# Expert token places resized: 800, 800, then 832, 800, 800, 768, 768, 768 by size

## The chip, the cores and the metric

The kernel runs on one core of one Trainium2 chip. The metric is the device time of one execution in microseconds (us); less is better. Before the change the median of three runs is 593.02 us (591.11 to 594.56).

## The reference, cut to what matters

Two stages follow each other. The first is a linear-attention recurrence over 768 steps for 4 batches and 8 heads of width 48; its output, 3072 tokens of 384 numbers, is the input `x` of the second. The second is a mixture of 8 experts:

```
logits = x @ w_gate
noisy_logits = logits + log1p(exp(x @ w_noise)) * noise
top2 = the two largest experts of each token, weights by a softmax over the two
for e in range(8):
    h = np.maximum(x[mask] @ w1[e], 0.0)          # 384 -> 1024
    out[mask] += top2_w * (h @ w2[e])             # 1024 -> 384
```

So 6144 pairs of token and expert are spread over 8 experts, 768 on average. The numbers per expert depend on the data. For the inputs that the reference draws with its default seed, its own routing gives 791, 781, 778, 777, 779, 765, 726 and 747 for experts 0 to 7.

## The kernel before, in words

The attention works on 24 tiles of 128 tokens; routing (logits, top two, the place of each token within its expert) follows in two groups of 13 and 11 tiles and is interleaved with it. From some 145 us on, the experts run one after the other.

Each expert has a fixed number of places. Tokens are gathered into these places by an indirect DMA from `xd` (the attention's output in DRAM), so every expert computes its places whether a token fills them or not. Experts 0 and 1 are handled as they are numbered, because their lists are ready early. The other six are sorted by token count on the chip (`ranks`, L905) and handled largest first; I call the eight positions **slots** 0 to 7. `N_TAIL` (L84) and `NS` (L87) give the places: six tiles of 128 for each slot, and for the first `8 - NS` slots a seventh, narrow tile (the **tail**) of 64 or 32.

A slot is worked in two chunks: chunk 0 has tiles 0 to 2, chunk 1 has tiles 3 to 5 and the tail where there is one (`CHUNKS1`, `CHUNKS2`). I write (slot, chunk), so (5,1) is the second chunk of slot 5. Each chunk goes through:

- `xgather` (L967): one indirect DMA per tile, issued by GpSimd, reads the tokens' rows.
- `spread` (L987): for slots 2 to 7, 16 DMAs on SP's queue rearrange the gathered rows into `xq`.
- `xT` (L1026): transposes the rows (slots 0 and 1 on TensorE at L1044, slots 2 to 7 on VectorE at L1037) and splits them into a high part `xh` (ScalarE, L1046) and a low part `xl` (VectorE, L1047).
- `p1` (L1053), the first matrix: for each of 8 blocks of hidden units (f = 0 to 7) nine matmuls at L1071 into one PSUM tile `ph`, 72 per chunk. The weights are the stationary operand, 128x128; the tokens of the whole chunk are the moving operand, so a matmul has 384, 416 or 448 columns. ScalarE (L1075) and VectorE (L1077) evict `ph` into `hb` for the full tiles and into `ht` for the tail.
- `p2` (L1083), the second matrix, tile by tile. A full tile takes 24 matmuls at L1107. A tail takes 16, eight each at L1098 and L1100; there the tokens are the stationary operand and the 384 outputs the moving columns. ScalarE copies the result out (L1115; for a tail L1102, with a VectorE add at L1103).
- `emit_out` (L1118): weighs by the gate, adds what the token's other expert gave (`pv`, gathered by `pgather`, L978) and scatters the rows to `out` by an indirect DMA (L1130).

The order of work on every engine is written out by hand: the loop at L1370 emits `p1` of a chunk with the next chunk's `spread` and gate work between its blocks, then `p2` with the next chunk's `xT` and weight loads between its tiles. In `p1` of a slot's last chunk, `w_p1` (L346) converts the next slot's weights; in `p2`, `w_p2` (L357) loads more. While chunk (0,1) runs, leftover routing work sits between its blocks: `one` (L624), whose matmuls L615 yield expert 1's list; `rows` (L805) turns the list into row numbers `GR` at L810; `tokens` (L812) follows, then `ranks`, `places` and `half` for the sorted six.

Tokens beyond an expert's places are counted in `tile_counts` (L939) against `cap`. If any count is above zero, the branch at L1433 redoes the excess with a slow loop over all experts (`slow_expert`, L872), which reads each expert's two weight matrices again.

Of the kernel before, what the change touches and what calls it, by code (L numbers as in the profile page):

```python
# [41 lines left out]
ESP = 2  # L42
# [12 lines left out]
def kernel(  # L55
# [14 lines left out]
    nc = tc.nc  # L70
    B, H, S, D = r.shape
    N, E = noise.shape
# [8 lines left out]
    CAP = 832  # L81
    NM = 6
    TAIL = CAP - NM * 128
    N_TAIL = (TAIL,) * 3 + (TAIL // 2,) * 3  # L84
    CHUNKS1 = ((0, 1, 2), (3, 4, 5, 6))
    CHUNKS2 = ((0, 1, 2), (3, 4, 5))
    NS = 2  # L87
    WMAX = 3 * 128 + TAIL
    EARLY = 384
    LS = 4096  # L90
# [141 lines left out]
    cap = const.tile([1, E], F32, name="cap")  # L232
# [21 lines left out]
    def consts_a():  # L254
        nc.vector.tensor_scalar(ltri, idif, 0.0, None, op0=ALU.is_gt)
        nc.gpsimd.memset(ones_b, 1.0)
        nc.gpsimd.memset(acc, 0.0)
        for t in vd + Z:
            nc.gpsimd.memset(t[:, :, D:], 0.0)
        for t in xs:  # L260
            nc.gpsimd.memset(t[:, DM:], 0.0)
        nc.gpsimd.iota(ie, pattern=[[1, E]], base=0, channel_multiplier=0, allow_small_or_imprecise_dtypes=True)
        nc.vector.tensor_scalar(ier, ie, -1.0, float(E), op0=ALU.mult, op1=ALU.add)
        nc.vector.tensor_scalar(ie_n[:, 0, :], ie, float(LS), None, op0=ALU.mult)
        nc.gpsimd.memset(dl, 0.0)
        nc.gpsimd.memset(cap, float(CAP))
        nc.gpsimd.memset(cap[:, 3:], float(NM * 128 + TAIL // 2))
        nc.gpsimd.memset(cap[:, E - NS:], float(NM * 128))
        nc.vector.tensor_copy(pid[:, 0, :], ie[:1])
        nc.gpsimd.iota(im, pattern=[[1, 128]], base=0, channel_multiplier=0)  # L270
        nc.gpsimd.iota(ij, pattern=[[LS // 128, E], [1, NJ]], base=0, channel_multiplier=0)
        nc.gpsimd.iota(pcol, pattern=[[0, 1]], base=0, channel_multiplier=1, allow_small_or_imprecise_dtypes=True)
        nc.gpsimd.iota(thi, pattern=[[1, NT]], base=1, channel_multiplier=0, allow_small_or_imprecise_dtypes=True)

        nc.vector.tensor_copy(imp, im)
        nc.vector.tensor_copy(ijp, ij.rearrange("p e j -> p (e j)")[:, :NJ])
# [213 lines left out]
    def xtrans(i):  # L490
        pt = psum.tile([128, ND, 128], F32, name="ptx", tag="py0")
        for d in range(ND):
            nc.tensor.transpose(pt[:, d, :], X[i][:, d * 128:(d + 1) * 128], ident)  # L493
        t = att_pool[0].tile([128, ND, 128], F32, name="xT", bufs=LB)
        nc.scalar.activation(t, pt, AF.Copy)
        XT[i] = t
# [3 lines left out]
    def logits(i):  # L500
        g = [i >= a for a, _ in GROUPS].count(True) - 1
        j = i - GROUPS[g][0]
        if j == 0:
            LG[g] = att_pool[0].tile([128, GB, 2 * E], F32, name="lg")
        if j % LB < LB - 1 and i + 1 < GROUPS[g][1]:
            return
        m = j % LB + 1
        pl = psum.tile([128, 2, 128], F32, name="pl", tag="pt", bufs=2)
        for d in range(ND):
            for a in range(m):  # L510
                nc.tensor.matmul(pl[32 * a:32 * a + 32, 0, :], wg[:, d, :], XT[i - m + 1 + a][:, d, :],  # L511
                                 start=(d == 0), stop=(d == ND - 1), skip_group_check=True)
        ys = att_pool[0].tile([128, 128], F32, name="ys", bufs=1)
        nc.scalar.activation(ys[:32 * m], pl[:32 * m, 0, :], AF.Copy)
        PL[i] = pl, ys, m

    def logits_b(i):
        if i not in PL:
            return
        pl, ys, m = PL.pop(i)  # L520
        g = [i >= a for a, _ in GROUPS].count(True) - 1
        j = i - GROUPS[g][0]
        nc.tensor.transpose(pl[:, 1, :32 * m], ys[:32 * m], ident[:32 * m, :32 * m])
        nc.scalar.activation(LG[g][:, j - m + 1:j + 1, :],
                             pl[:, 1, :32 * m].rearrange("p (a b) -> p a b", b=32)[:, :, :2 * E], AF.Copy)
# [413 lines left out]
    def tile_counts(cnt, capped):  # L939

        nt = const.tile([1, E], F32, name="nt")
        if capped:
            nc.vector.tensor_sub(nt, cnt, cap)
            cnt = nt
        nc.vector.tensor_scalar(nt, cnt, 127.0, None, op0=ALU.add)
        nc.vector.tensor_add(nt[:, 0:1], nt[:, 0:1], ie_n[:1, 0, 0:1])
        nc.vector.tensor_scalar(nt, nt, 0.0, 1.0 / 128.0, op0=ALU.max, op1=ALU.mult)
        nc.vector.tensor_scalar(nt, nt, -127.0 / 256.0, 12582912.0, op0=ALU.add, op1=ALU.add)
        nc.vector.tensor_scalar(nt, nt, -12582912.0, None, op0=ALU.add)
        nc.vector.tensor_scalar(nt, nt, float(NCH), float(NCH), op0=ALU.mult, op1=ALU.min)  # L950
        nc.vector.tensor_copy(tab[:, :E], nt)
        mx = const.tile([1, 1], F32, name="mx")
        nc.vector.tensor_reduce(mx, nt, AX.X, ALU.max)
        nc.vector.tensor_add(mx, mx, bad)
        nc.vector.tensor_copy(tab[:, E + 1:E + 2], mx)


    def tw(e, t):
        return N_TAIL[e] if t == NM else 128

    XG, XH, HH, PV, OT, scat_of = {}, {}, {}, {}, {}, {}
    def chunks(e):
        return CHUNKS1 if e < E - NS else CHUNKS2

# [175 lines left out]


    consts_a()
    uterm_a(0)
    prep_k(1)
# [225 lines left out]
    for s in range(1, len(seq)):  # L1370
        e, ci = seq[s]
# [61 lines left out]
    with tc.If(any_r > 0):  # L1433
        thr = slow.tile([128, E], F32, name="thr")
        for e in range(E):
            nc.vector.memset(thr[:, e:e + 1], float(CAP if e < 3 else NM * 128 + (TAIL // 2 if e < E - NS else 0)))
        bad_r = nc.values_load(tab[:, E:E + 1], min_val=0, max_val=1)
        with tc.If(bad_r > 0):
            att_pool[0] = slow
            eye = slow.tile([D, D], F32, name="eye")  # L1440
            nc.vector.tensor_copy(eye, ident[:D, :D])
            one_d = slow.tile([D, 1], F32, name="one_d")
            nc.vector.memset(one_d, 1.0)
            with tc.For_i(0, B, 1) as b:
                with tc.For_i(0, H, 1) as h:
                    slow_head(b, h, slow, eye, one_d)
            nc.sync.dma_start(out.rearrange("(q p) d -> p q d", p=128),
                              zrow[:, None, :].to_broadcast([128, N // 128, DM]))
            nc.vector.memset(acc, 0.0)
            nc.vector.memset(ie_n[:, 0, 0:1], 0.0)  # L1450
            for i in range(NT):
                c, b = divmod(i, B)
                X[i] = slow.tile([128, DM], F32, name="xs")
                nc.sync.dma_start(X[i], xd[i * 128:(i + 1) * 128, :DM])
                xtrans(i)
                logits(i)
                logits_b(i)
                for g in range(len(GROUPS)):
                    if GROUPS[g][1] == i + 1:
                        for _ in route(g, False):  # L1460
                            pass
            pc = pwarm[:, 432:432 + E]
            nc.tensor.matmul(pc, ones_b, acc, start=True, stop=True)
            tile_counts(pc[:1], False)
            nc.vector.memset(tab[:, E:E + 1], 1)
            nc.vector.tensor_copy(pid[:, 0, :], ie[:1])
            nc.vector.memset(thr, 0.0)
        gov = slow.tile([128, E * NT], F32, name="gov")
        for e in range(E):
            g = slow.tile([128, 2, NT], F32, name="ge")  # L1470
            nc.vector.tensor_scalar(thr[:, e:e + 1], thr[:, e:e + 1], float(e * LS), None, op0=ALU.add)
            nc.vector.tensor_scalar(g, SLI, thr[:, e:e + 1], None, op0=ALU.is_ge)
            nc.vector.scalar_tensor_tensor(g, SLI, float((e + 1) * LS), g, op0=ALU.is_lt, op1=ALU.mult)
            nc.vector.tensor_mul(g, g, GTS)
            nc.vector.tensor_add(gov[:, e * NT:(e + 1) * NT], g[:, 0], g[:, 1])
        with tc.For_i(0, E, 1) as e:
            slow_expert(e, slow, gov)
# [29 lines left out]
```

## Time and profile before

| | before |
|---|---|
| runs, us | 593.02, 591.11, 594.56 |
| span of the profiled execution, first to last instruction, us | 590.2 |
| TensorE busy (matmul / weight load) | 572.8 us (97%) / 537.6 us (91%) |
| VectorE, ScalarE, GpSimd busy | 364.3, 254.4, 275.0 us |
| L1071, first matrix, 1152 matmuls | three groups of some 132 us each |
| L1107, second matrix, 1152 matmuls | 199.8 + 129.0 us |
| DMA | 85.45 MB, mean 145 GB/s |

The profile gives one execution and its span; a time of that execution beside its span isn't given, so the span stands beside the runs. The span is 2.8 us under their median. Matmuls are pipelined and their ends are modelled: a matmul's own duration includes latency, and the pitch from one start to the next says what it costs. The lists by line say where the time sits; the chain of waits says which of it sets the end.

### The profile page before, as it was taken

How to read it: one execution, taken by the hardware profiler on the slowest of the kernel's cores; microseconds unless marked ns; L12 is line 12 of the kernel's file. 1: busy time of each engine (PE TensorE's matmuls, PEld its weight loads, DVE VectorE, ACT ScalarE, POOL GpSimd, SP SyncE). 2: the span in 40 equal slices, each digit the busy share in tenths (PEclk: the TensorE clock that was granted, in tenths of full speed). 3: DMA queues.
4: the chain of work that ended last, by engine and by line, in shares of the span. 5: the costliest groups of instructions: out<-in, count | busy, mean ns of one | idle time of the engine just before them, and what ended most of it. 6: DMA issues, size and time to landing. Idle time of an engine off the chain costs nothing.

```text
span 590.2 us, 12599 instructions
## 1 busy us (share of the span) xinstructions
PE 572.8 (97%) x4502; PEld 537.6 (91%) x4503; DVE 364.3 (62%) x858; ACT 254.4 (43%) x641; POOL 275.0 (47%) x413
## 2 busy tenths in 40 slices
PE   8999998998999999999999999999999999999995
PEld 5888887876989999999999999999999999999994
DVE  8777769997969985636373646445363735455330
ACT  3777777665225251524342434325243524434220
POOL 7886766853026365145532623370454226235102
PEclk9999999999999999999999999999999999999999
DMA  7999876966123356456553835473565538454101
GB/s 133 212 216 246 191 175 154 233 183 188 73 52 121 95 164 161 117 150 157 156 162 105 207 117 155 125 201 107 163 163 151 160 100 202 124 156 118 46 15 40
DMA packets 134091, 85.45 MB, mean 145 GB/s; under 512 B 109715, under 2 KB 124148, under 8 KB 134021
## 3 DMA queue, kind: packets, MB, share of 16 engines
q1 hardware_dynamic: 124292, 56.43, 38.6%
q0 software_dynamic: 9728, 28.14, 16.4%
q8 instruction: 37, 0.61, 0.4%
q14 instruction: 34, 0.27, 0.2%
HBM read 58.14 MB, written 19.51 MB: 132 GB/s over the span
## 4 chain that ended last, share of the span: by engine, by line
PE 88%; DVE 6%; issue 2%; DMA 1%; ACT 1%; POOL 1%; POOLq 0%; DVEq 0%; ACTq 0%
PE ph L1071 35%; PE pym L1107 32%; PE pa L414 4%; PE yt L467 3%; PE pt L402 2%; PE ptx L493 2%; PE yt L455 1%; PE pym L1098 1%; PE pym L1100 1%; PE ptb L476 1%; PE pwarm L430 1%; DMA xg<-xd,GR 1%; PE pl L511 1%; DVE am L421 1%; PE pwarm L166 1%
## 5 line engine op out<-in xcount | busy, mean ns | idle before, releaser
L1107 PE MATMUL pym<-w1h,hb 128*128 128x384 f32 x768 | 199.8, 336 | 0.0
L1107 PEld LDWEIGHTS pym<-w1h,hb 128*128 128x128 f32 x768 | 139.0, 188 | 0.2
L1071 PE MATMUL ph<-xh,w0h 128*128 128x384 f32 (+2 forms) x384 | 133.1, 347 | 0.0
L1071 PE MATMUL ph<-xl,w0h 128*128 128x384 f32 (+2 forms) x384 | 132.3, 345 | 0.4 <-DVE xl L1047 0.4
L1071 PE MATMUL ph<-xh,w0l 128*128 128x384 f32 (+2 forms) x384 | 132.0, 344 | 0.0
L1107 PE MATMUL pym<-w1l,hb 128*128 128x384 f32 x384 | 129.0, 336 | 0.0
L1077 DVE SCALAR_TENSOR_TENSOR hb<-ph,hb 128x384 fp32r<-128x384 f32 x128 | 71.1, 556 | 91.7 <-ACT hb L1075 45.1
L1130 POOL DMA_INDIRECT out_dram<-ot,TK x54 | 55.8, 1034 | 141.2 <-DVE ot L1126 121.2
L1075 ACT ACTIVATE hb<-ph 128x384 fp32r<-128x384 f32 x128 | 63.0, 492 | 102.7 <-PE ph L1071 102.0
L1071 PEld LDWEIGHTS ph<-xl,w0h 128*128 128x128 f32 x384 | 72.1, 188 | 1.8 <-DVE xl L1047 0.6
L1071 PEld LDWEIGHTS ph<-xh,w0h 128*128 128x128 f32 x384 | 72.1, 188 | 1.7 <-issue 0.2
L1071 PEld LDWEIGHTS ph<-xh,w0l 128*128 128x128 f32 x384 | 72.2, 188 | 1.3
L973 POOL DMA_INDIRECT xgt<-xd,GR x40 | 42.0, 1051 | 65.4 <-DMA xq<-xgt 17.3
L1107 PEld LDWEIGHTS pym<-w1l,hb 128*128 128x128 f32 x384 | 72.1, 188 | 0.0
L982 POOL DMA_INDIRECT pv<-out_dram,GA x47 | 53.2, 1132 | 28.0 <-issue 15.6
L1115 ACT ACTIVATE ot<-pym 128x384 f32<-128x384 f32 x39 | 19.2, 492 | 92.6 <-PE pym L1107 85.0
L396 ACT ACTIVATE cv<-vd,c 128x48 f32<-128x48 f32 x176 | 44.0, 324 | 0.1
L421 DVE TENSOR_TENSOR am<-pa,mneg 128x512 int32<-128x512 int32 x48 | 32.7, 684 | 16.6 <-PE pa L414 16.4
L1047 DVE TENSOR_TENSOR xl<-xq,xh 128x384 fp32r<-128x384 f32 (+2 forms) x40 | 21.3, 532 | 34.7 <-ACT xh L1046 34.7
L369 POOL TENSOR_TENSOR kd<-kt,tabk 128x192 f32<-128x192 f32 x46 | 28.9, 649 | 11.8 <-DMA kt<-in_k_dram 5.4
L1046 ACT ACTIVATE xh<-xq 128x384 fp32r<-128x384 f32 (+2 forms) x40 | 20.0, 500 | 32.7 <-DVE xq L1037 30.5
L1126 DVE SCALAR_TENSOR_TENSOR ot<-ot,GT,pv 128x384 f32<-128x384 f32 (+2 forms) x44 | 26.4, 610 | 11.8 <-ACT ot L1115 11.8
(300 smaller groups left out, 812.9 us busy)
## 6 DMA issues: line engine op xcount, KB each, us to landing
stg<-in_moe_w_dram SPq DMA_DIRECT2D x32, 384.0 KB, 3.5
stg<-in_moe_w_dram SPq DMA_DIRECT2D x72, 128.0 KB, 4.4
xq<-xgt SPq DMA_DIRECT2D x172, 36.0 KB, 1.9
rd<-in_r_dram SPq DMA_DIRECT2D x24, 192.0 KB, 4.0
vd<-in_v_dram SPq DMA_DIRECT2D x24, 192.0 KB, 3.7
out_dram<-zrow SPq DMA_DIRECT2D x16, 288.0 KB, 3.7
kt<-in_k_dram SPq DMA_DIRECT2D x23, 192.0 KB, 3.6
stg<-in_moe_w_dram SPq DMA_DIRECT2D x6, 512.0 KB, 5.5
```

The source lines that it names most:

```text
L369: (eng or nc.gpsimd).tensor_mul(kd[i % 3][:, h, :D], kt[i][:, h], tabk[:, h, :D])
L396: nc.scalar.activation(CV[i][:, h, :], vt[i][:, h, :], AF.Copy, scale=C8[i][:, h, :])
L414: nc.tensor.matmul(pa[s][:, p, :], kT[i][s * 64:(s + 1) * 64, p, :], rT[i][s * 64:(s + 1) * 64, p, :], start=True, stop=True)
L421: nc.vector.tensor_tensor(AM[i][:, s].bitcast(I32), PA[i][s].bitcast(I32), mneg.to_broadcast([128, NP, 128]), op=ALU.bitwise_and)
L973: nc.gpsimd.indirect_dma_start(out=xg[:n], out_offset=None, in_=xd[:GROUPS[GEARLY - 1][1] * 128] if early_ else xd, in_offset=bass.Indirec ...
L982: nc.gpsimd.indirect_dma_start(out=pv[:n], out_offset=None, in_=out, in_offset=bass.IndirectOffsetOnAxis(ap=GA[:n, e * NJ + t:e * NJ + t + ...
L1071: nc.tensor.matmul(ph[:, :w_], a[:, d, fs], x[:, :w_ // 32, d], start=(j == 0), stop=(j == len(q) - 1))
L1075: nc.scalar.activation(h_[:, f, 0, :], ph[:, a:b], AF.Relu)
L1077: nc.vector.scalar_tensor_tensor(h_[:, f, 1, :], ph[:, a:b], 0.0, h_[:, f, 0, :].bitcast(F32), op0=ALU.max, op1=ALU.subtract)
L1107: nc.tensor.matmul(py, hb[:, f, a, hs], x[:, f, :], start=(j == 0), stop=(j == len(q) - 1))
L1126: nc.vector.scalar_tensor_tensor(ot[:n], pt[:n], g, PV[e, t][:n], op0=ALU.mult, op1=ALU.add)
L1130: st = nc.gpsimd.indirect_dma_start(out=out, out_offset=bass.IndirectOffsetOnAxis(ap=TK[:n, q:q + 1], axis=0), in_=ot[:n], in_offset=None, ...
```

## The change

The place counts move from 832, 832, 832, 800, 800, 800, 768, 768 to 800, 800, 832, 800, 800, 768, 768, 768. So the tails of slots 0 and 1 shrink from 64 to 32, slot 2 keeps 64, slots 3 and 4 keep 32, and slot 5 loses its tail of 32. The limits used for counting the excess and for the slow branch follow.

```
-    N_TAIL = (TAIL,) * 3 + (TAIL // 2,) * 3
+    N_TAIL = (TAIL // 2, TAIL // 2, TAIL, TAIL // 2, TAIL // 2)
...
-    NS = 2
+    NS = 3
...
-        nc.gpsimd.memset(cap, float(CAP))
-        nc.gpsimd.memset(cap[:, 3:], float(NM * 128 + TAIL // 2))
+        nc.gpsimd.memset(cap, float(NM * 128 + TAIL // 2))
+        nc.gpsimd.memset(cap[:, ESP:ESP + 1], float(CAP))
         nc.gpsimd.memset(cap[:, E - NS:], float(NM * 128))
...
-            nc.vector.memset(thr[:, e:e + 1], float(CAP if e < 3 else NM * 128 + (TAIL // 2 if e < E - NS else 0)))
+            nc.vector.memset(thr[:, e:e + 1], float(NM * 128 + (N_TAIL[e] if e < E - NS else 0)))
```

## Rows read from the trace of the kernel before

**Rows 1.** The page: span, busy time of each engine, clock granted to TensorE.

```profile
span 590.2 us, 12599 instructions
PE 572.8 (97%) x4502; PEld 537.6 (91%) x4503; DVE 364.3 (62%) x858; ACT 254.4 (43%) x641; POOL 275.0 (47%) x413
...
PEclk9999999999999999999999999999999999999999
```

**Rows 2.** Everything TensorE waited for from 174 us on: total, times, longest.

```profile
PE ptm L1044 <- DMA xg<-xd,GR: 0.4, 1, 0.4
```

**Rows 3.** Chain that ended last, in order of time: start us, us, what.

```profile
174.74 9.14 PE ph L1071 x45
...
235.49 14.66 PE ph L1071 x72
...
265.52 12.53 PE ph L1071 x72
...
345.60 13.62 PE ph L1071 x72
...
374.55 12.49 PE ph L1071 x72
...
453.53 13.62 PE ph L1071 x72
...
482.48 12.49 PE ph L1071 x72
...
507.46 12.48 PE ph L1071 x72
...
532.43 12.59 PE ph L1071 x72
...
583.48 0.51 POOLq L1432
```

**Rows 4.** Instructions in order, TensorE: tails of (1,1) and (5,1), next matmul.

```profile
262.56 0.34 PE L1098 MATMUL pym<-w1h,ht 128*128 128x384 f32 x1
...
265.35 0.34 PE L1071 MATMUL ph<-xh,w0h 128*128 128x384 f32 x1
...
479.56 0.33 PE L1098 MATMUL pym<-w1h,ht 128*64 128x384 f32 x1
...
482.32 0.34 PE L1071 MATMUL ph<-xh,w0h 128*128 128x384 f32 x1
```

**Rows 5.** Instructions in order, VectorE, chunk (0,1): start, duration, [idle before <- releaser].

```profile
179.06 0.56 DVE L1077 SCALAR_TENSOR_TENSOR hb<-ph,hb 128x384 fp32r<-128x384 f32 x1 [0.64 <-ACT ht L1075]
...
189.19 0.17 DVE L810 TENSOR_SCALAR GR<-lt 128x7 int32<-128x7 f32 x1
```

**Rows 6.** Instructions that write `ht`: line engine op count, duration ns min/median/max, starts, forms.

```profile
L1077 DVE SCALAR_TENSOR_TENSOR ht<-ph,ht x48: 179/196/216, 177.7 to 468.3; 128x64 fp32r<-128x64 f32 x24, 128x32 fp32r<-128x32 f32 x24
```

**Rows 7.** The gather behind it: chain in order of time, then TensorE's instruction.

```profile
191.48 3.10 DMA xg<-xd,GR
...
194.62 0.55 PE L1044 MATMUL ptm<-ident,xg 128*128 128x128 f32 x3 [0.37 <-DMA xg<-xd,GR]
```

**Rows 8.** Instructions in order, chunks (1,1) and (5,1): VectorE, GpSimd, SP's queue.

```profile
256.95 0.56 DVE L1047 TENSOR_TENSOR xl<-xq,xh 128x384 fp32r<-128x384 f32 x1 [0.59 <-ACT xh L1046]
...
473.95 0.56 DVE L1047 TENSOR_TENSOR xl<-xq,xh 128x384 fp32r<-128x384 f32 x1 [0.59 <-ACT xh L1046]
...
485.80 0.89 POOL L1130 DMA_INDIRECT out_dram<-ot,TK  x1 [0.23 <-issue]
...
464.67 5.14 SPq L323 DMA_DIRECT2D stg<-in_moe_w_dram  x3
474.54 10.25 SPq L995 DMA_DIRECT2D xq<-xgt  x16
```

**Rows 9.** Chunk (6,0): us, busy PE, PEld, DVE, ACT, POOL; clock, DMA share, GB/s.

```profile
482.50:507.50 25.00, 25.00 (x146) 25.00 (x146) 13.21 (x24) 9.06 (x18) 14.28 (x17) 1.00 0.64 164
```

**Rows 10.** The page: what DMA moved in 40 slices of the span.

```profile
GB/s 133 212 216 246 191 175 154 233 183 188 73 52 121 95 164 161 117 150 157 156 162 105 207 117 155 125 201 107 163 163 151 160 100 202 124 156 118 46 15 40
```

## The prediction

> **What bounds the kernel now.** I read the page's busy shares first: TensorE is busy 97% of a span of 590.2 us, no other engine over 62%, and its granted clock is full in all 40 slices [rows 1]. A busy share alone proves little, so the second view is TensorE's waits. From 174 us to the end it waited once, 0.4 us [rows 2]. The third view, the chain of waits in order of time, agrees: from 235 us on it is an unbroken run of L1071 and L1107, each piece starting where the one before ends [rows 3]. So after 174 us a matmul that goes away shortens the kernel by its pitch, as long as what feeds TensorE keeps up.
>
> **What a narrower chunk is worth.** The chain has chunks of all three widths, so the prices need no model. 72 matmuls of L1071 take 14.66 us at 448 columns, 13.62 at 416, 12.48 to 12.59 at 384 [rows 3]: some 1.05 us for every 32 columns. The tail in the second matrix is another matter. Its 16 matmuls take 482.32 - 479.56 = 2.76 us with 32 tokens and 265.35 - 262.56 = 2.79 with 64 [rows 4], because the tokens are the stationary operand there and 384 columns pass in either case. Halving a tail saves only in the first matrix; removing it saves both.
>
> **Slot 5, tail removed.** It loses 32 columns in p1 and the 16 tail matmuls in p2. A slot that has just this shape already runs: chunk (6,1) goes from 507.46 to 532.43, 24.97 us, where (5,1) goes from 453.53 to 482.48, 28.95 [rows 3]. Saved: **3.98 us**. Off the path, this also removes one gather of `xgt`, one of `pv` and one scatter, each near 0.9 us of GpSimd by the scatter's row [rows 8], and 8 evictions of `ht` on ScalarE and 8 on VectorE, the latter 0.18 us each, the shortest of their kind [rows 6], with the copy, the additions and the split of that one tile. SP still issues 16 spread DMAs; only their sizes fall. What hides the feeding work, and by how much? The next chunk's last `xl` is written at 473.95 + 0.56 = 474.5, and TensorE starts on it at 482.3 [rows 4, 8]. That is 7.8 us of slack, and an arrival some 4 us sooner uses about half. The weights of slot 6 that `p1` of (6,0) converts are issued by 464.67 + 5.14 = 469.8 [rows 8], over 12 us ahead. SP's 16 spread DMAs for (6,1) end their issue at 484.8 [rows 8], and `p2` of (6,0), which holds the transposes that read them, begins at 482.48 + 12.49 = 494.97 [rows 3], or 491 after the change; 6 us remain. On GpSimd the `pv` gathers of slot 6 stand behind slot 5's last scatter, from 485.80 [rows 8]. That scatter is the tail's, so it goes, and the one before it comes earlier with its tile; they move along with TensorE. I take the full 3.98. From below it is bounded by the tail matmuls alone, 2.76; above, nothing else is there to save.
>
> **Slot 1, tail from 64 to 32.** Chunk (1,1) lasts from 235.49 to 265.52, 30.03 us; (3,1), with the new width, from 345.60 to 374.55, 28.95 [rows 3]. Saved: **1.08 us**. The cover is `xl` of the next chunk, ready at 257.5, and TensorE gets to it at 265.35 [rows 4, 8]: 7.8 us of slack against one.
>
> **Slot 0, tail from 64 to 32.** Chunk (0,1) starts at 174.74 [rows 3] and gets the same 1.08 us in p1, but here TensorE isn't alone. Its one wait, 0.37 us at 194.62, is for a gather of expert 1's rows that lands at 191.48 + 3.10 = 194.58 [rows 7]. That gather waits for `GR`, written by VectorE at L810 at 189.19 [rows 5]. Between 179.06 and there the view shows no idle time of VectorE ahead of any of the 24 instructions after the first (the group has the first and the last of these 25 rows): evictions, leftover routing and weight conversion stand in one line, and the last wait that let it start was the eviction of f = 1 at 179.06 [rows 5]. So p1's end doesn't set the gather; VectorE's line does. With 416 columns that line starts earlier by two of the eight blocks, 2 x 1.08 / 8 = 0.27 us, and by some 0.03 in ScalarE's eviction of `ht`; its own six `ht` evictions up to L810 shrink from 0.21 to 0.18 (the longest and the shortest of `ht`) [rows 6], 6 x 0.03 = 0.18. Together 0.48 us. TensorE would reach the transpose 1.08 us sooner and wait about 0.95 us in place of 0.37. Saved: **0.48 us**. The bounds are 0, if the gather doesn't move, and 1.08, if it keeps pace. The smaller tails of slots 0 and 1 also make gathers, scatters and three TensorE transposes cheaper; I cost these at nothing: they only get smaller, and the wait at 194.62 sits behind them [rows 7].
>
> **The rest.** The memsets of `cap` stay three, in the first microseconds, where GpSimd's place in the line doesn't change. Slot 5's missing tile shifts the alternation of two PSUM banks and the rings of `ot` and `pv` by one; each reuse distance stays.
>
> **The sum.** 3.98 + 1.08 + 0.48 = 5.54 us. Against the span, 590.2 becomes 584.7. The median of the runs, 593.02, lies 2.8 us above the span; I leave that as it is: 593.0 - 5.5 = **587.5 us**, 0.93% less.
>
> **A rule against this.** TensorE's weight loads are busy 91% of the whole span and all 25.00 us of a 384-wide chunk [rows 1, 9]. If weight loading were the limit, narrower chunks would win nothing in p1 and only the tail's 2.76 us would remain: 593.0 - 2.8 = 590.2. The Trainium skill (Trainium Kernel Development and Optimization, section Performance Expectations) calls matmul busy time a bad measure and the busy share of LDWEIGHTS a good one, which is a reading that would point this way. The rows speak against it: with the same 128x128 loads the stretch of 72 falls from 14.66 to 13.62 to 12.5 us as columns fall [rows 3], and the change goes below 384 nowhere.
>
> **Rivals.**
> - *Weight loads bind*: as just said, 590.2. Chance 0.02.
> - *The feeders of slot 6 become the bound.* With slot 5's tail gone, 4 us of TensorE work that covered SP's spread and GpSimd's gathers are missing. For it: these are serial lines of 10 us on SP [rows 8]. Against: 6 to 8 us of slack, and (6,1) to (7,0) runs in the same shape without a wait [rows 2, 3]. It decides where more than that slack is lost; then up to 4 us come back: 591.5. Chance 0.05.
> - *The places don't suffice.* This is the side on which it gets slower. It decides at 801 tokens in expert 0 or 1, or 769 in the sixth slot. Routing the reference's default inputs gives 791 and 781, and sorted 779, 778, 777, 765, 747, 726, against 800, 800 and 832, 800, 800, 768, 768, 768. The nearest are 3 tokens away, so here it holds; other data could break it. Then the branch at L1433 runs, which the chain shows not taken (it ends at L1432's load [rows 3] and no instruction of the branch is recorded). It would read 8 x 3.15 = 25.2 MB of weights again; at 246 GB/s, the best slice [rows 10], that is 102 us, so 690 us at least. Chance 0.02.
> - *Slot 0 keeps all or nothing*: 586.9 or 588.0. This is inside my forecast, and only the profile can tell.
>
> **How the numbers follow.** The forecast has 0.91. Its terms run from 0 + 1.0 + 3.9 = 4.9 to 1.08 + 1.08 + 3.98 = 6.1 us saved, so 586.9 to 588.1; the three runs before scatter by about 1.7 us to either side, and that sets the range more than the terms do: 585.2 to 589.8. 0.5%, about what a measurement of this kernel can tell from no change, is 3.0 us, so faster means below 590.05. Faster: the forecast, less a little for scatter, 0.90. Same: weight loads, late feeders and scatter, 0.07. Slower: places that don't suffice and what I have not seen, 0.03.
>
> **What would show it.** In the profile of the changed kernel the chain should have L1071 x72 pieces of about 13.6 us for chunk (1,1) and 12.5 for (5,1), and chunk (5,1) should last 25.0 us. L1098 and L1100 should count 40 each in place of 48. TensorE's wait at L1044 near 194 should grow to about 0.95 us; if it stays 0.4, slot 0 kept its microsecond. No other wait should appear after 174 us. I am wrong if a new wait of TensorE stands at the start of (6,0), if (5,1) takes over 26 us, or if anything under L1433 runs.

## The result, and the profile after

Four runs of each: **587.87 us** after (586.91 to 589.73), 593.41 before (591.11 to 594.56). The ratio is 0.9915, 95% interval 0.9888 to 0.9942: 5.54 us less, with 5.5 forecast. The profiled execution of after took 589.73 us with a span of 588.0, so 1.7 us lie around the span.

The page of after (span, busy times, TensorE's clock in 40 slices), against [rows 1]:

```profile
span 588.0 us, 12519 instructions
...
PE 570.0 (97%) x4486; PEld 535.8 (91%) x4487; DVE 360.9 (61%) x844; ACT 252.5 (43%) x631; POOL 271.5 (46%) x409
...
PEclk9999999899899999999999999999999999999999
```

TensorE is busy as large a share as before. The spans differ by 2.2 us only. The clock line shows two slices early on below full. By windows of after (us; busy time and count of PE, PEld, DVE, ACT, POOL; clock, DMA share, GB/s):

```profile
100.00:110.00 10.00, 8.29 (x103) 6.56 (x102) 7.77 (x22) 4.21 (x16) 7.35 (x14) 0.83 0.73 180
140.00:150.00 10.00, 8.33 (x45) 5.95 (x44) 7.52 (x27) 3.50 (x10) 2.84 (x3) 0.74 0.63 178
150.00:160.00 10.00, 10.00 (x66) 10.00 (x66) 8.39 (x34) 2.95 (x6) 0.00 (x0) 0.92 0.21 80
```

The lower of the two clock levels (1.2 of 2.4 GHz) was granted for some 10 us in these windows, before the first narrower chunk; in the kernel before it was 1.00 in all three. The first matmul of (0,1) starts at 178.27 us; before it was 174.58. That 3.69 us is this execution's own (an execution of the change further below has it at 174.14), so I compare chunk by chunk from there on. The chain of after in order of time (start us, us, what), against [rows 3]:

```profile
238.19 13.59 PE ph L1071 x72
251.78 12.57 PE pym L1107 x72
267.11 12.49 PE ph L1071 x72
...
455.07 12.61 PE ph L1071 x72
467.68 12.58 PE pym L1107 x72
480.25 12.53 PE ph L1071 x72
492.79 12.51 PE pym L1107 x72
505.29 12.48 PE ph L1071 x72
517.77 12.49 PE pym L1107 x72
530.26 12.59 PE ph L1071 x72
```

A chunk lasts from one start of L1071 to the next. (1,1) takes 267.11 - 238.19 = 28.92 us, with 13.59 in p1; (5,1) takes 480.25 - 455.07 = 25.18, with 12.61 in p1. In us, from the first matmul of each chunk:

| chunk | before | after | change | forecast |
|---|---|---|---|---|
| (0,1) | 32.45 | 31.59 | -0.86 | -0.48 |
| (1,0) | 28.30 | 28.16 | -0.14 | 0 |
| (1,1) | 30.03 | 28.93 | -1.10 | -1.08 |
| (5,1) | 28.95 | 25.19 | -3.76 | -3.98 |
| (6,0) | 24.98 | 25.04 | +0.06 | 0 |
| (0,1) to the end | 415.52 | 409.66 | -5.86 | -5.54 |

The other chunks agree within 0.06 us. All that TensorE waited for from 178 us on, in after (total, times, longest), against [rows 2]:

```profile
PE ptm L1044 <- DMA xg<-xd,GR: 0.5, 1, 0.5
```

The instruction that waited (start, us, what, [idle before <- releaser]), against [rows 7]:

```profile
197.39 0.55 PE L1044 MATMUL ptm<-ident,xg 128*128 128x128 f32 x3 [0.50 <-DMA xg<-xd,GR]
```

One wait as before, grown from 0.37 to 0.50 us; nothing new at (6,0). The tail matmuls count 40 where 48 were (line, shapes, count, busy us, mean ns, idle before):

```profile
L1098 PE MATMUL pym<-w1h,ht 128*64 128x384 f32 (+1 forms) x40 | 13.4, 336 | 0.0
L1100 PE MATMUL pym<-w1l,ht 128*32 128x384 f32 (+1 forms) x40 | 13.4, 336 | 0.0
```

### The profile page after: what moved, and what is told of

Its sections match the earlier page's. It is cut to its first block, busy times and chain, and to the rows that moved or that the text cites. A ratio compares the mean times of both kernels' runs of the same rounds, so it can differ in the third digit from the quotient of the medians.

```text
span 588.0 us, 12519 instructions
## 1 busy us (share of the span) xinstructions
PE 570.0 (97%) x4486; PEld 535.8 (91%) x4487; DVE 360.9 (61%) x844; ACT 252.5 (43%) x631; POOL 271.5 (46%) x409
## 4 chain that ended last, share of the span: by engine, by line
PE 87%; DVE 6%; issue 2%; DMA 2%; ACT 1%; POOL 1%; SPq 0%; POOLq 0%; DVEq 0%; ACTq 0%
PE ph L1071 34%; PE pym L1107 32%; PE pa L414 4%; PE yt L467 3%; PE pt L402 2%; PE ptx L493 2%; PE yt L455 1%; PE pl L511 1%; PE pym L1098 1%; PE pym L1100 1%; PE ptb L476 1%; DMA xg<-xd,GR 1%; PE pwarm L430 1%; DVE am L421 1%; DMA rd<-in_r_dram 1%
## 5 line engine op out<-in xcount | busy, mean ns | idle before, releaser
L1107 PE MATMUL pym<-w1h,hb 128*128 128x384 f32 x768 | 199.8, 336 | 0.0
L1107 PEld LDWEIGHTS pym<-w1h,hb 128*128 128x128 f32 x768 | 138.9, 188 | 0.1
L1071 PE MATMUL ph<-xh,w0h 128*128 128x384 f32 (+2 forms) x384 | 133.1, 347 | 0.0
L1071 PE MATMUL ph<-xl,w0h 128*128 128x384 f32 (+2 forms) x384 | 131.9, 343 | 0.0
L1071 PE MATMUL ph<-xh,w0l 128*128 128x384 f32 (+2 forms) x384 | 131.7, 343 | 0.0
L1077 DVE SCALAR_TENSOR_TENSOR hb<-ph,hb 128x384 fp32r<-128x384 f32 x128 | 71.1, 556 | 94.2 <-ACT hb L1075 56.7
L1107 PE MATMUL pym<-w1l,hb 128*128 128x384 f32 x384 | 128.9, 336 | 0.0
L1075 ACT ACTIVATE hb<-ph 128x384 fp32r<-128x384 f32 x128 | 63.0, 492 | 102.2 <-PE ph L1071 100.6
L1071 PEld LDWEIGHTS ph<-xh,w0h 128*128 128x128 f32 x384 | 72.7, 189 | 1.2 <-issue 0.4
L1071 PEld LDWEIGHTS ph<-xh,w0l 128*128 128x128 f32 x384 | 72.7, 189 | 0.5
L1071 PEld LDWEIGHTS ph<-xl,w0h 128*128 128x128 f32 x384 | 72.8, 190 | 0.4
L1107 PEld LDWEIGHTS pym<-w1l,hb 128*128 128x128 f32 x384 | 72.1, 188 | 0.0
```

What stands on the lines that cost most here:

```text
L1071: nc.tensor.matmul(ph[:, :w_], a[:, d, fs], x[:, :w_ // 32, d], start=(j == 0), stop=(j == len(q) - 1))
L1075: nc.scalar.activation(h_[:, f, 0, :], ph[:, a:b], AF.Relu)
L1077: nc.vector.scalar_tensor_tensor(h_[:, f, 1, :], ph[:, a:b], 0.0, h_[:, f, 0, :].bitcast(F32), op0=ALU.max, op1=ALU.subtract)
L1107: nc.tensor.matmul(py, hb[:, f, a, hs], x[:, f, :], start=(j == 0), stop=(j == len(q) - 1))
```

## The experiments

Twelve runs in three sets. The kernel before ran beside each: 598.06 us (median of 20), 596.56 (12) and 592.48 (11). Sets 1 and 2 ran on one chip, set 3 on another, and this matters below: on the first of them the kernel before itself is some 3 to 6 us slower than on the other or in the first comparison (593.41). The diffs are against the changed kernel unless they say otherwise; `...` marks lines left out, most of them the limits for counting, which follow the place counts.

### The parts alone

Slot 5's edit alone (set 1, diff against the kernel before):

```
-    N_TAIL = (TAIL,) * 3 + (TAIL // 2,) * 3
+    N_TAIL = (TAIL,) * 3 + (TAIL // 2,) * 2
...
-    NS = 2
+    NS = 3
...
```

> Only slot 5 loses its tail; slots 0 and 1 keep 64. Theory (TensorE's path sets the time, each part is worth its matmuls): chunk (5,1) lasts 25.2 us as in the changed kernel, against 28.95 before; chunk (0,1) is 32.4 us as before, with TensorE's wait at L1044 at 0.4 us; the time falls by 3.8 us (ratio 0.9936). Rival (slot 6's feeders become late): a wait of TensorE at the start of (6,0), and less than 2 us gained. Rival (the gain needs all parts together): the time moves by less than 2 us.

Measured: 591.85 us, ratio 0.9919 (0.9889 to 0.9949); (5,1) 25.19, (1,1) unchanged at 30.03. So slot 5 carries the larger part of the gain. The medians are 6.2 us apart where 3.8 were expected; the kernel before was not profiled on this chip, so where the rest lies stays open.

Slots 0 and 1 alone (set 1, against the kernel before):

```
-    N_TAIL = (TAIL,) * 3 + (TAIL // 2,) * 3
+    N_TAIL = (TAIL // 2, TAIL // 2, TAIL) + (TAIL // 2,) * 3
...
```

> Only the tails of slots 0 and 1 go from 64 to 32; slot 5 keeps its tail. Theory: (0,1) lasts 31.6 us (32.45 before) with a wait of 0.5 us at L1044, (1,1) 28.9 us (30.03 before), (5,1) 28.95 as before; together 2.0 us less (ratio 0.9967). Rival (VectorE's line takes all of slot 0's gain): (0,1) stays at 32.4 and the sum is 1.1 us. Rival (weight loads bind TensorE): no gain at all, since no tail tile goes.

Measured: 596.86 us, ratio 0.9981 (0.9953 to 1.001). (1,1) came to 28.93 as expected, but (0,1) to 34.42, longer than the 32.45 of the kernel before in the first comparison. That miss is taken up below.

The change without slot 0's part (set 3):

```
-    N_TAIL = (TAIL // 2, TAIL // 2, TAIL, TAIL // 2, TAIL // 2)
+    N_TAIL = (TAIL, TAIL // 2, TAIL, TAIL // 2, TAIL // 2)
...
-        nc.gpsimd.memset(cap[:, ESP:ESP + 1], float(CAP))
+        nc.gpsimd.memset(cap[:, 0:ESP + 1:ESP], float(CAP))
```

> The change with slot 0's tail left at 64 tokens, so that (0,1) has 448 columns again; slots 1 and 5 as in the change. Theory (on this chip 416 columns in (0,1) let the late signal grow until VectorE's line makes TensorE wait and the clock falls to half, 34.4 us): (0,1) is 33.3 us without half clock in it, (1,1) 28.93, (5,1) 25.19, and the time is 1.2 us below that of the change in the same set of runs, about 592. Rival (what the profiles of (0,1) show is chance): (0,1) is 34 us or more here too, and the time is 1.0 us above that of the change, since the 448 columns are paid for.

Measured: 587.25 us, ratio 0.9916 (0.9899 to 0.9932); (0,1) 32.48, (1,1) 28.93, (5,1) 25.19. The change itself had 585.86 in the same runs and (0,1) 31.69. So slot 0's 32 places are worth 0.79 us by the profiles and 1.39 by the medians. The theory's 33.3 us did not come; the rival had the sign right, but not with its 34 us.

### What sets (0,1)

The changed kernel again (set 2):

> The changed kernel itself, beside the kernel before on the same chip as the next three. Theory: chunk (0,1) to (1,0) 31.6 us, (1,1) 28.9, (5,1) 25.2, and 5.5 us less in the time (ratio 0.991). Rival (part of the gain was scatter of the first comparison): the ratio lies above 0.995.

Measured: 593.3 us, ratio 0.9967 (0.993 to 1.0004): less gain than in the first comparison. (1,1) and (5,1) are the known 28.93 and 25.19, but (0,1) takes 34.44. Its instructions in order: ScalarE, VectorE, then TensorE:

```profile
187.85 0.49 ACT L1075 ACTIVATE hb<-ph 128x384 fp32r<-128x384 f32 x1 [3.84 <-remote]
...
188.47 0.56 DVE L1077 SCALAR_TENSOR_TENSOR hb<-ph,hb 128x384 fp32r<-128x384 f32 x1 [2.38 <-ACT ht L1075]
...
187.55 0.35 PE L1071 MATMUL ph<-xh,w0l 128*128 128x416 f32 x1
189.62 0.42 PE L615 MATMUL pwarm<-xq 128*128 128x14 bf16 x11 [1.72 <-DVE xq L611]
...
191.11 0.55 PE L1071 MATMUL ph<-xh,w0h 128*128 128x416 f32 x1
191.46 0.55 PE L1071 MATMUL ph<-xl,w0h 128*128 128x416 f32 x1
```

Here is a chain of delays. ScalarE's eviction of f = 4 waits 3.84 us, though TensorE's next blocks run on to 187.55. VectorE, next in line, stands 2.38 us, is late with L611, and TensorE waits 1.72 at L615. Right after that its clock is at half (0.50 from 189.87 to 193.28 us): the pitch from 191.11 to 191.46 is 0.35 us, where full clock gives some 0.19. All seven profiles of the first two sets with 416 columns in (0,1) show ScalarE's wait, 3.1 to 4.4 us long, ending 11.9 to 12.0 us after the chunk's first matmul, and TensorE's wait of 1.6 to 1.7 us at L615. In five of them the clock fell to half within 1.6 us of that wait's end; in two (the additions and the 352 columns below) it stayed full there.

The view names ScalarE's releaser "remote", that is, no recorded update fits it. That proves little: this profile holds 8888 semaphore updates, the same kernel's in set 3 has 11632, and the other profiles of the first chip lack about as many. No instruction fetch lies between 172.9 and 190.7 us, and no DMA packet from 183 to 189 us took more than 0.61. What holds the signal back stays open. It isn't a matter of (0,1) alone either: in (1,0) of this execution ScalarE waits 3.74 us at 217.27, and the chunk takes 29.66 us in place of 28.17. Each of the seven profiles has (1,0) or (2,0) longer by 1.4 us or more.

Set 3, on the other chip, has the kernel before as a control and the change once more.

> The kernel before, profiled on the chip of the other runs, as a control. In the first comparison its chunk (0,1) lasted 32.45 us with 448 columns; the run of slot 5's edit alone, which has the same 448 columns there, had 33.27 us here with the clock at full. Theory (the late signal to ScalarE in (0,1) belongs to this chip or these executions, and at 448 columns it costs some 0.8 us): (0,1) is 33.1 to 33.5 us, ScalarE waits over 1 us there at L1075, (1,1) is 30.03 and (5,1) 28.95. Rival (the late signal comes with the changed program alone): (0,1) is 32.4 us and ScalarE waits under 0.6 us. A second rival (it strikes any program at random): (0,1) is 34 us or more, with the half clock in it.

> The change itself, as the reference for the two others in the same runs. Theory (416 columns in (0,1) bring the late signal on this chip): (0,1) 34.4 us with 3.4 us of half clock in it, (1,1) 28.93, (5,1) 25.19, a ratio to the kernel before of 0.9915 to 0.997. Rival (chance): (0,1) is near 31.6 us as in the first comparison, and the ratio 0.991 or less.

Measured: the kernel before 592.92 us (one run), (0,1) 32.49, ScalarE's longest wait at L1075 1.2 us, each for TensorE. The change 585.86 us, ratio **0.9893** (0.9874 to 0.9913), (0,1) 31.69, no half clock in it and no "remote". So neither the program alone nor chance from one execution to the next brings the late signal: it was in every such profile on one chip and in none on the other or in the first comparison. The kernel before was not profiled on the first of these chips, so what (0,1) costs there with 448 columns was seen only in the one profile of slot 5's edit: 33.27.

The TensorE instruction that waited, in the control and then in the change, both of set 3:

```profile
195.71 0.55 PE L1044 MATMUL ptm<-ident,xg 128*128 128x128 f32 x3 [0.39 <-DMA xg<-xd,GR]
```

```profile
193.36 0.55 PE L1044 MATMUL ptm<-ident,xg 128*128 128x128 f32 x3 [0.61 <-DMA xg<-xd,GR]
```

The wait grows by 0.22 us, and the chunk shortens by 0.80: together 1.02, near the 1.06 us by which p1 shortened (15.02 to 13.96 from its first matmul to the first of p2).

Is it VectorE's line that sets the gather? Two additions put into it, ahead of `rows` (set 2):

```
     def listed_1():
+        for _ in range(2):
+            nc.vector.tensor_add(zrow, zrow, zrow)
         rows(NJ, ESP * NJ)
```

> The changed kernel with two extra VectorE additions (128x384, 0.5 us each by rows of that shape) in front of the row numbers GR of expert 1 in chunk (0,1). Theory (VectorE's line sets when expert 1's rows arrive, and TensorE waits for them): TensorE's wait at L1044 grows by 1.0 us to 1.5, and (0,1) lasts 32.6 us in place of 31.6. Rival (TensorE's own end of the first matrix sets the gather, VectorE has slack): the wait stays 0.5 and (0,1) stays 31.6.

Measured, one run, 597.48 us; (0,1) 36.84 against 34.44 in the change of that set. VectorE's and TensorE's instructions:

```profile
192.36 1.15 DVE L1349 TENSOR_TENSOR zrow<-zrow 128x384 f32<-128x384 f32 x2
...
193.62 0.17 DVE L810 TENSOR_SCALAR GR<-lt 128x7 int32<-128x7 f32 x1
...
197.65 0.55 PE L1044 MATMUL ptm<-ident,xg 128*128 128x128 f32 x3 [1.48 <-DMA xg<-xd,GR]
198.96 0.90 PE L1044 MATMUL ptm<-ident,xg 128*128 128x128 f32 x3 [0.76 <-DMA xg<-xd,GR]
```

`GR` came 17.54 us after the chunk's first matmul (193.62 - 176.08), 0.87 later than in the change of that set (192.55 - 175.88 = 16.67), and TensorE waited 1.48 and 0.76 at L1044. VectorE's line does set the gather; the end of p1 does not, for it came 1.5 us sooner here than in that change (15.77 us after the chunk's first matmul, not 17.31). The chunk grew by 2.40 us, more than the additions' 1.15, and nearly all of it is the two waits, 2.24 us, where the change of that set had none at L1044: there TensorE came later, since its clock was at half in p1. Here the clock stayed full in p1 and was at half from 198.9 to 202.3, behind the waits.

### Odd and even slots

The odd slots' weights, which have a pool of their own (`wts1`), moved by 192 bytes in SBUF (set 1); the buffers of the pool `late` behind them (`xgt`, `xq`, `pv`), which even and odd slots share, move along:

```
     att_stack.close()
+    padp = stack.enter_context(tc.tile_pool(name="padp", bufs=1, side="right"))
+    pad = padp.tile([128, 48], F32, name="pad")
+    nc.gpsimd.memset(pad[:, :1], 0.0)
     wts1 = stack.enter_context(tc.tile_pool(name="wts1", bufs=1, side="right", reuse_waits="tile"))
```

> The changed kernel, the odd slots' weights moved by 192 bytes in SBUF, so that they start at the same offset within 4096 bytes as the even slots' weights. Question: in both profiles 72 matmuls of an odd slot take 12.58 to 12.61 us and those of an even one 12.48 to 12.53. If the offset of the weights sets this, odd slots fall to 12.49 us and the kernel gains some 8 x 2 x 0.09 = 1.4 us (ratio to before 0.988). If it is the half of SBUF, or something else that alternates with the slot, odd slots stay at 12.58 to 12.61 and the time is that of the changed kernel (0.9915).

Its chain in order of time, chunks (5,0), (5,1) and (6,0):

```profile
432.55 12.48 PE ph L1071 x72
445.04 12.49 PE pym L1107 x72
457.52 12.48 PE ph L1071 x72
470.00 12.49 PE pym L1107 x72
482.49 12.48 PE ph L1071 x72
```

The odd slot 5 now runs like the even 6: 12.48 and 12.49 us where after had 12.61 and 12.58 (455.07 and 467.68 above). The even slots, with their weights unmoved, kept their 12.48 and 12.49. The place of the weights sets it: 0.1 us per 72 matmuls, 1.3 to 1.8 ns for one. Which part of the address matters wasn't tried. The time, 593.71 us, ratio 0.9937 (0.9903 to 0.9971), didn't show the sum of it; (0,1) had the late signal, 34.17 us, and (1,0) took 29.76.

All tails at 32 (set 1), which narrows slot 2 as well:

```
-    N_TAIL = (TAIL // 2, TAIL // 2, TAIL, TAIL // 2, TAIL // 2)
+    N_TAIL = (TAIL // 2,) * 5
...
```

> The changed kernel with slot 2's tail also cut from 64 to 32 (800 places for slots 0 to 4; the largest count of the sorted six is 779). Theory: the 72 matmuls of L1071 in (2,1) fall from 14.61 to 13.55 us, (2,1) from 29.88 to 28.82, nothing else moves: 1.06 us under the changed kernel, 6.6 us under the kernel before (ratio 0.9889). Rival (feeders of slot 3 late): (2,1) is followed by a wait.

Measured: 592.7 us, ratio 0.9912 (0.9884 to 0.9941). (2,1) fell from 29.87 to 28.83, as its width says. This profile also has (2,0) at 28.82 instead of 25.0, with an idle stretch of 1.8 us and half clock behind it, so the time cannot confirm the sum.

The pieces that paid, put together (set 3): slot 0 kept at 64, slots 1 to 4 at 32, and the pad above.

```
-    N_TAIL = (TAIL // 2, TAIL // 2, TAIL, TAIL // 2, TAIL // 2)
+    N_TAIL = (TAIL,) + (TAIL // 2,) * 4
...
```

> The best pieces together: slot 0's tail kept at 64, slots 1 to 4 at 32, slots 5 to 7 without, and the odd slots' weights moved by 192 bytes. Theory (all pieces add): against the change, (2,1) loses 1.05 us, the odd slots 3, 5 and 7 some 0.1 to 0.2 per chunk or 1.1 in all, and (0,1) 1.2, so 3.3 us less than the change in the same runs, about 590 here. Rival (the waits and half-clock stretches ahead of slot 2 take it back, as they did where the pieces stood alone): (1,0) or (2,0) are 1.5 us longer, and the time is that of the change or at most 1 us less.

Measured: **583.86 us** (583.32 to 584.22), ratio 0.9853 (0.9834 to 0.9873). This beats both kernels, by 8.6 us and, in the same runs, by 2.0. Its chain in order of time, p1 of (1,1), (2,1) and (5,1) with what follows:

```profile
235.11 13.55 PE ph L1071 x72
248.66 12.49 PE pym L1107 x72
...
288.91 13.55 PE ph L1071 x72
302.45 12.49 PE pym L1107 x72
...
450.31 12.48 PE ph L1071 x72
462.79 12.49 PE pym L1107 x72
```

(2,1) lost 1.04 us, and the odd chunks (1,1), (3,0), (3,1), (5,0), (5,1), (7,0) 0.10 to 0.22 each, 1.03 in all. From the start of (0,1) to the end it takes 407.17 us, the change 410.00. Of these 2.83 us another 0.83 lie in (7,1), whose length differs by 0.7 among the three profiles of the change alone. The 1.2 us expected from slot 0 rested on the late signal, which this chip lacks. Still, (0,1) took 31.89 us with its 448 columns, not 32.48 as in the run without slot 0's part: TensorE does not wait at L1044. `GR` is no sooner, but GpSimd starts the first gather 0.45 us after it (189.54, 189.99) and not 0.98; the other run with the pad shows 0.45 too, every run without it 0.98. Why is open. Slot 0 kept at 64 probably costs here, since the run without slot 0's part lost time; the same kernel with 32 there too wasn't run.

### The rivals of the forecast

Do weight loads bind? In slots 6 and 7, 64 of the 72 matmuls of p1 get 352 columns instead of 384 (set 2):

```
-                nc.tensor.matmul(ph[:, :w_], a[:, d, fs], x[:, :w_ // 32, d], start=(j == 0), stop=(j == len(q) - 1))
+                wn = 352 if e >= 6 and j else w_
+                nc.tensor.matmul(ph[:, :wn], a[:, d, fs], x[:, :wn // 32, d], start=(j == 0), stop=(j == len(q) - 1), skip_group_check=True)
```

> The changed kernel; in slots 6 and 7, 64 of the 72 matmuls of L1071 in each chunk pass 352 columns in place of 384 (the last 32 places of these chunks get one of their nine products). Theory (columns set the pitch down to there too): 14.5 ns less for each, 0.93 us per chunk, so L1071's 72 take 11.6 us, 3.7 us less in all. Rival (the weight loads, 128 columns each, bind at 384): they stay at 12.5 us and nothing is gained.

Chain of that kernel in order of time, p1 of (6,1) and (7,0) (L1072 is L1071 of the others):

```profile
510.40 11.71 PE ph L1072 x72
...
534.62 11.62 PE ph L1072 x72
```

The window of p1 of (6,1) (columns as in the windows above):

```profile
510.00:522.00 12.00, 12.00 (x76) 12.00 (x75) 7.82 (x13) 7.49 (x12) 1.32 (x3) 1.00 0.42 116
```

p1 fell from 12.48 and 12.59 us to 11.71 and 11.62, by 0.77 and 0.97, near the 0.93 that 64 narrower matmuls give at 1.05 us for 72; the other two chunks lost 0.81 and 0.87. The time was 591.89 us, one run. PEld is busy for all 12.00 us of the window and still does not set the pitch. The Trainium skill (Trainium Kernel Development and Optimization, section Performance Expectations) names the busy share of LDWEIGHTS, beside MFU (the share of the peak arithmetic rate), as a good measure of how close a kernel is to its roofline. Here it reads 100% while fewer columns, with as many loads, still save time; so a full share does not show that the loads bind.

What does it cost when the places don't suffice? Slot 4 with 768 places for its 777 tokens (set 2):

```
-    N_TAIL = (TAIL // 2, TAIL // 2, TAIL, TAIL // 2, TAIL // 2)
+    N_TAIL = (TAIL // 2, TAIL // 2, TAIL, TAIL // 2)
...
-    NS = 3
+    NS = 4
```

> The changed kernel with slot 4's tail taken away too: 768 places for 777 tokens, so 9 tokens exceed their places and the slow branch runs. Theory of the prediction's slower rival: 4 us saved in (4,1), and at least 102 us added by reading 25.2 MB of weights again, so 690 us at least; with the branch's own matmuls for the one expert that has an excess, 700 to 1200. Rival (the branch is cheap because only 9 tokens are redone): under 600 us.

Measured: 1162.72 us, ratio 1.9452 (1.9287 to 1.9617). By line, TensorE in the stretch from 595 to 1160 us (line, shapes, count, busy us, mean ns, idle before and its releasers):

```profile
L896 PE MATMUL s_ph<-s_xt,s_w 128*128 128x128 f32 x1152 | 178.6, 330 | 15.6 <-DVE s_xt L891 15.6
L901 PE MATMUL s_py<-s_w,s_h 128*128 128x384 f32 x384 | 127.8, 486 | 0.0
L889 PE MATMUL s_px<-ident,s_xg 128*128 128x128 f32 x72 | 15.3, 331 | 187.6 <-DMA s_pv<-out_dram 118.5 <-DMA s_xg<-xd 69.1
```

The branch takes some 564 us ((7,1) to the end is 596.69 us, 32.2 without it), for nine tokens. (4,1) itself saved 3.86 us; but (5,0) and (6,0) took 31.77 and 29.86 us in place of 25.17 and 25.04, TensorE waiting 3.7 and 1.9 us at L1107 for ScalarE's evictions, one of which had waited 8.1 us at L1075. So what this tail is worth without the late signal stays open.

## Why the prediction was right, and where its steps were off

- **The bound.** Right: in the two undisturbed pairs of profiles what falls off TensorE's stream comes off the time from (0,1) to the end, one for one but for the wait at L1044 (5.86 us here; 415.47 - 410.00 = 5.47 in set 3, where (7,1) came out 0.30 longer).
- **The sum.** That the medians moved by just the 5.54 us of the sum is luck in part: slot 5 gave 0.22 less than forecast, slot 0 gave 0.38 more and (1,0) 0.14 that was not in it, and the runs scatter by more than that.
- **Slot 1, 1.08 us.** Measured 1.10: (1,1) takes 28.93 in every run that had the edit, 28.83 with the pad.
- **Slot 5, 3.98 us.** Measured 3.76. The step at fault is the model "a slot that has just this shape already runs": I took (6,1), an even slot, for slot 5, an odd one. [rows 3] had the sign of it, 12.59 at 532.43 for (7,0) against 12.48 at 507.46 for (6,1). I noted that spread as "12.48 to 12.59" and didn't ask what it followed. (7,0), 25.16 us, would have given 3.79. The shifted weights show the cause.
- **Slot 0, 0.48 us.** Measured 0.86 (first pair) and 0.80 (set 3). The step at fault is the shrinkage of VectorE's line. The line's start came 0.28 us sooner after the chunk's first matmul, 0.30 forecast. But from there to `GR` it shortened by 0.57, from 10.13 us [rows 5] to 9.56, where I allowed 0.18 for the `ht` evictions. In after:

```profile
182.47 0.56 DVE L1077 SCALAR_TENSOR_TENSOR hb<-ph,hb 128x384 fp32r<-128x384 f32 x1 [0.51 <-ACT ht L1075]
...
189.22 0.26 DVE L611 TENSOR_SCALAR xq<-xq,pcol 128x77 bf16<-128x77 bf16 x1
189.38 0.54 DVE L1077 SCALAR_TENSOR_TENSOR hb<-ph,hb 128x384 fp32r<-128x384 f32 x1
...
192.03 0.17 DVE L810 TENSOR_SCALAR GR<-lt 128x7 int32<-128x7 f32 x1
```

  The same place before, with ScalarE's eviction of `ht` ahead of it, and then that eviction in after:

```profile
186.12 0.22 ACT L1075 ACTIVATE ht<-ph 128x64 fp32r<-128x64 f32 x1
...
186.12 0.26 DVE L611 TENSOR_SCALAR xq<-xq,pcol 128x77 bf16<-128x77 bf16 x1
186.37 0.56 DVE L1077 SCALAR_TENSOR_TENSOR hb<-ph,hb 128x384 fp32r<-128x384 f32 x1
```

```profile
189.02 0.19 ACT L1075 ACTIVATE ht<-ph 128x32 fp32r<-128x32 f32 x1
```

  L1077 starts 0.16 us after L611 in after; before it was 0.25. The next L1077, behind a weight conversion, shows the same: 1.13 us after the start of L344 against 1.21. Before, both start 0.03 us after ScalarE's eviction has ended (186.12 + 0.22 = 186.34, then 186.37), as at 179.06, where the view does name ScalarE as what ended the wait. In after it is 0.17 and 0.16 us, and L1077 follows its own engine's work. The pair of set 3 agrees. So the view's "no idle time" hid short waits for ScalarE: before, the line was still paced in part by p1, against "VectorE's line does" in the prediction. One short instruction, L638, took 0.32 us before and 0.16 after. With the 0.18 these make 0.51 of the 0.57. The wait at L1044 therefore grew to 0.50, not 0.95.
- **(1,0), not forecast:** 0.14 us less, in set 3 by 0.09. It goes with slot 1's edit (28.16 in the run without slot 0's part, 28.30 in slot 5's alone). The prediction put the smaller transposes of the tail at nothing; they give some 0.03 of it (the first one's pitch fell from 0.11 to 0.08), the rest is open.
- **The rest at nothing.** Right: no new wait in after. Weight loads as the bound fell with the 352 columns; late feeders with (6,0) at 25.04. The places suffice; the price of the other side, put at 102 us at least from the weights alone, is some 564, because the branch waits for gathers and runs 1608 matmuls.
- **The base.** I made the sum against the span and kept the 2.8 us to the median. The execution of after shows 1.7 us around its span, so some 1.1 of the 2.8 was scatter among runs.
- **How far it carries.** 0.9915 and 0.9893 agree with the sum of 5.54 (0.9907). 0.9967 on the chip with the late signal doesn't: there (0,1) took 34.4 us with the narrower tail, against 33.27 in the one profile with 448 columns, and (1,0) 29.66 against 28.30, which takes back part of the gain.

## What to carry to other kernels

Where one engine's stream is unbroken, look for a stretch in the trace that already has the new shape, and take it from the same buffers (here the same parity of slot): a spread of 1% between equal stretches had a cause here and was not noise. For a line of short instructions on another engine, "no idle time" in a view does not mean that nothing paces it; compare starts, not the idle column. And where a size is cut close to the data, price the fallback by running it.

## What was not expected of the hardware

- The place of the stationary operand in SBUF changes a matmul's pitch: 72 at 384 columns took 12.59 to 12.61 us in an odd slot, 12.48 with the weights moved by 192 bytes, as in an even slot.
- On one chip ScalarE waited 3.1 to 4.4 us for TensorE's signal at the same point of every profile with 416 columns in (0,1); on another, never. The cause is open.
- After a wait of 1.72 us TensorE's clock was at half from 189.87 to 193.28 us, at a cost of 1.6 us (nine matmuls in 3.33 us instead of 1.69): the stall and the slow stretch together cost about twice the stall. The length of the wait does not settle it: in two profiles the clock stayed full behind waits of 1.66 and 1.67 us at the same instruction.
